# Attention in a fused kernel: value products in three blocks per pair of heads instead of five, and what uses their sums half a step later

## The chip, the cores and the metric

The kernel runs on one core of one Trainium2 chip. TensorE (PE), VectorE (DVE), ScalarE (ACT), GpSimd (POOL) and SyncE (SP, which issues DMAs) each work through their own instruction list in order; where one needs what another makes, it waits on a semaphore. The metric is the device time in microseconds (us) of one execution.

## The reference, cut to what matters

Attention with a bias computed from positions feeds a layer of experts and a gated layer. Only the attention is touched by the change.

```python
scores = scale * np.matmul(q, k.transpose(0, 1, 3, 2))      # 4 batches, 8 heads, 576 x 576
scores = scores + bias.transpose(2, 0, 1)[None, :, :, :]
scores = scores - np.max(scores, axis=-1, keepdims=True)
attn = np.exp(scores)
attn = attn / (np.sum(attn, axis=-1, keepdims=True) + 1e-09)
return np.matmul(attn, v).astype(np.float32)
...
x = np.ascontiguousarray(attn_out.transpose(0, 2, 1, 3)).reshape(B * S, H * D)
x = _moe_ref(x=x, **moe_kwargs)
return _moe2_ref(x=x, **moe2_kwargs)
```

## The kernel before

A first stage computes the bias and writes it to DRAM, the attention stage follows, and then come the experts and the gated layer. The attention works on pairs of heads, 16 of them: pair 0 to pair 15, four for each batch. A pair has five **steps** (0 to 4), one for each block of 115 query rows. The loop runs over `u` in twos; step k of pair P is `u = 10 P + 2 k`, so `u % 10 // 2` is k. Its code is written out in one order, and that order is the order on every engine. A step issues:

1. On PE the score products of the *next* step (`emit_qk`, 12 matmuls into two `sc` banks).
2. For the step itself the transposes of the weights after exp: four into bank `pa` and three into `pb` (`emit_T`); ACT copies both to the buffers `ptt` (`emit_pte`).
3. For the next step, on DVE, bias and row minimum (`emit_max`, two instructions at line 351, which read the `sc` banks), then on ACT two exps (`emit_exp`).
4. `service(u)`: one item of the list `fill`.
5. Value products from the list `avq`: so many blocks of keys as `AVN[k]` says.
6. Two more transposes into `pa`, once ACT has emptied it, and ACT's copy of them; the next step's four transposes into `pa` wait for this copy.
7. `service(u + 1)`: one more item of `fill`.

**Value products.** The rows of a pair are taken in two groups, g = 0 (230 rows, steps 0 and 1) and g = 1 (346 rows, steps 2 to 4). A group has five blocks of keys, c = 0 to 4 (`emit_av`, two products of 64 output rows each, into bank `av`); after the last one DVE copies the sum (line 397). Group 0 is queued at the end of step 1, group 1 at the end of step 4, so that it is worked off in steps 0 and 1 of the next pair. Behind its last block four items are put on `fill`:

- `x_back(P, 0)`: four transposes of the sums into bank `mi`, then on DVE two small operations on the row sums (lines 410, 411) and a multiply that reads `mi` (line 417).
- `x_back(P, 1)`: one transpose into `mi`, a multiply, and the DMAs of the result.
- `x_fwd(P, 0)`, `x_fwd(P, 1)`: four transposes and one, each with a copy on DVE (434, 437).

At step 4 `prep` puts items for the pair after next on `fill`: two times four transposes (`tr_main`, line 198, copied by DVE at 201 and 203), one transpose with the loads of later pairs (`tr_rem`), and two items that only POOL works on (`split_pair`: a copy, line 216, and a subtraction, line 218). There is one bank `mi`: each of these items waits until DVE has read what the one before left there.

**Where `fill` runs behind.** After the last pair of a batch three items for the router (`logits`) come in between, and one slot is given to the router's matmul. So in pairs 1 to 4, 8 and 12 `x_back(0)` stands at the end of step 1 (these are called *quick* pairs below), in pairs 5, 6, 9, 10, 13 and 14 at the end of step 2 (*late* pairs), in pairs 7 and 11 at the beginning of step 2 (*middle* pairs). The slots of a quick pair, two for each step: `tr_rem`, `split 0` | `split 1`, `x_back 0` | `x_back 1`, `x_fwd 0` | `x_fwd 1`, nothing | `tr_main 0`, `tr_main 1`.

The bias of a pair's two heads is read back from DRAM into `nb` by DMAs in the first pairs (`nb_load`); the loads for pair 3 are issued in pair 1, behind the other loads in SP's queue.

Of the kernel before, what the change touches and what calls it, by code (L numbers as in the profile page):

```python
# [19 lines left out]
B, H, S, D = 4, 8, 576, 64  # L20
# [9 lines left out]
NP = H // 2  # L30
# [17 lines left out]
def fused(ctx, tc, q, k, v, w1, b1, w2, wg, mw1, mw2, gw, vw, ow, rg, tab, cst, out):  # L48
# [21 lines left out]
    def bank(nm):  # L70
        return {"pa": ps_pt, "pb": ps_pt, "av": ps_av, "mi": ps_mi}[nm].tile([128, 512], F32, name=nm, tag=nm)
# [78 lines left out]
    with tc.manual_schedule():  # L150
# [24 lines left out]
        def load_pair(P):  # L175
            b, hp = divmod(P, NP)
            r = f0[:, 2 * S * (P % 2):2 * S * (P % 2) + 2 * S].rearrange("p (n h d) -> p n h d", h=2, d=D)
            for c, src in ((0, k), (1, q)):
                for i in range(2):
                    a = src[b, 2 * hp + i]  # L180
                    sy.dma_start(out=r[:, 4 * c:4 * c + 4, i], in_=bass.AP(a.tensor, a.offset, [[D, 128], [128 * D, 4], [1, D]]))
                    sy.dma_start(out=r[64 * c:64 * c + 64, 8, i], in_=a[512:576])
            raws[P] = r

        def load_v(P):
            b, hp = divmod(P, NP)
            vt = v_r[P % 3].rearrange("p (t h d) -> p t h d", h=2, d=D)
            for i in range(2):
                a = v[b, 2 * hp + i]
                sy.dma_start(out=vt[:, 0:4, i], in_=bass.AP(a.tensor, a.offset + 64 * D * i, [[D, 128], [128 * D, 4], [1, D]]))  # L190
                sy.dma_start(out=vt[64 * i:64 * i + 64, 4, i], in_=a[512 * (1 - i):512 * (1 - i) + 64])
            vts[P] = vt

        def tr_main(P, c):
            assert P == 0 or P - 1 in prepped
            p = bank("mi")
            for n in range(4):
                te.transpose(p[:, 128 * n:128 * n + 128], raws[P][:, 4 * c + n].rearrange("p h d -> p (h d)"), idF)
            o = kqf_r[P % 2][:, S * c:S * c + 512]
            if c == 0:  # L200
                ve.tensor_copy(o, p)
            else:
                ve.tensor_scalar(o, p, -0.125, None, ALU.mult)

        def tr_rem(P):
            p = bank("mi")
            te.transpose(p[:, 0:128], raws[P][:, 8].rearrange("p h d -> p (h d)"), idF)
            o = kqf_r[P % 2].rearrange("p (c s) -> p c s", c=2)
            ve.tensor_copy(o[:, 0, 512:576], p[:, 0:64])
            ve.tensor_scalar(o[:, 1, 512:576], p[:, 64:128], -0.125, None, ALU.mult)  # L210

        def split_pair(P, part):
            assert last_qk[0] >= 10 * P - 11
            x, kq = kqf_r[P % 2], kq_r[P % 2]
            if part == 0:
                ge.tensor_copy(kq[:, 0:2 * S], x)  # L216
            else:
                ge.tensor_tensor(kq[:, 2 * S:4 * S], x, kq[:, 0:2 * S].bitcast(F32), ALU.subtract)
                kqs[P] = [kq[:, S * c:S * c + S] for c in range(4)]
                prepped.add(P)  # L220

        def prep(P):
            return [
                lambda: tr_main(P, 0),
                lambda: tr_main(P, 1),
                lambda: (tr_rem(P), load_pair(P + 2) if 0 < P < B * NP - 2 else None, load_v(P) if P > 1 else None),
                lambda: split_pair(P, 0),
                lambda: split_pair(P, 1),
            ]


# [156 lines left out]
        def emit_av(P, g, c):  # L388
            n = NG[g]
            pt = pts[g]  # L390
            if c == 0:
                avs[P, g] = bank("av")
            a = avs[P, g]
            for i in range(2):
                te.matmul(a[64 * i:64 * i + 64, 0:n], vts[P][:, c, i], pt[8 if c == 4 else 4 * i + c], start=(c == 0), stop=(c == T - 1))  # L395
            if c == T - 1:
                ve.tensor_copy(xu_r[P % 2][:, NG[0] * g:NG[0] * g + n], a[:, 0:n])
                if g == 1:
                    fill.extend([lambda: x_back(P, 0), lambda: x_back(P, 1), lambda: x_fwd(P, 0), lambda: x_fwd(P, 1)])

        def fb(P, part):
            return "pa" if P == B * NP - 1 and part else "mi"
# [1 line left out]
        def x_back(P, part):  # L404
            b, hp = divmod(P, NP)
            r = P % 2
            t0, t1 = ((0, 4), (4, 5))[part]
            n = t1 - t0
            if part == 0:
                ve.tensor_scalar(rinv[:QP, r], sums[:QP, r], 1e-9, None, ALU.add)  # L410
                ve.reciprocal(rinv[:QP, r], rinv[:QP, r])
            xu = xu_r[r]
            xt = x_r[r].rearrange("p (t i d) -> p t i d", t=T, i=2)
            p = bank(fb(P, part))
            for t in range(t0, t1):
                te.transpose(p[:QP, 128 * (t - t0):128 * (t - t0) + 128], xu[:, QS * t:QS * t + QP], idF)
            ve.tensor_tensor(xt[:QP, t0:t1], p[:QP, 0:128 * n].rearrange("p (t i d) -> p t i d", t=n, i=2),
                             rinv[:QP, r, t0:t1].unsqueeze(3).to_broadcast([QP, n, 2, D]), ALU.mult)
            if part == 1:
                xt = x_r[r].rearrange("p (t d) -> p t d", t=T)  # L420
                dst = x_dr[b * S:(b + 1) * S, 128 * hp:128 * hp + 128]
                sy.dma_start(out=dst[0:T * QS].rearrange("(t p) d -> p t d", p=QS), in_=xt[:QS])
                sy.dma_start(out=dst[S - 1:S], in_=xt[QS:QP, T - 1])

        def x_fwd(P, part):
            b, hp = divmod(P, NP)
            xt = x_r[P % 2].rearrange("p (t d) -> p t d", t=T)
            o = xT[b % 2].rearrange("p (k s) -> p k s", s=S)[:, hp]
            p = bank(fb(P, part))
            pv = p.rearrange("p (c r) -> p c r", r=128)  # L430
            if part == 0:
                for t in range(4):
                    te.transpose(pv[:, t, 0:QP], xt[:QP, t], idF[:QP, :QP])
                ve.tensor_copy(o[:, 0:4 * QS].rearrange("p (t q) -> p t q", q=QS), pv[:, :, 0:QS])
            else:
                te.transpose(pv[:, 0, 0:QP], xt[:QP, 4], idF[:QP, :QP])
                ve.tensor_copy(o[:, 4 * QS:S], pv[:, 0, 0:QP])
                if hp == NP - 1:
                    sy.dma_start(out=xT_dr[b], in_=xT[b % 2])
                    fill.extend([lambda: logits(b), lambda: logits2(b, 0), lambda: logits2(b, 1)])  # L440
# [229 lines left out]
        U1 = 0  # L670
        EVD = ()
        FLN = (1,) * 10
        AVN = (3, 2, 2, 2, 1)
        fill, rq = [], []
        def service(u):
            Pn = u // 10 + 2
# [18 lines left out]
        for u in range(-2, NU, 2):  # L695
# [11 lines left out]
            service(u)  # L707
            for _ in range(min(len(avq), AVN[u % 10 // 2])):
                avq.pop(0)()
# [510 lines left out]
```

## Time and profile before

| what | value |
|---|---|
| time, median of 3 runs | 1095.11 us (1094.44 to 1096.6) |
| the profiled execution: its time, its span | 1097.88 us, 1096.1 us |
| bias stage, up to the first score products of pair 0 | 64.66 us |
| attention, up to the first product of the experts | 322.50 us; PE busy 310.04, ACT 219.66, DVE 201.84 |
| the rest | 708.94 us; PE busy 688.32 |
| granted TensorE clock, mean | 0.987 |

The span runs from the first to the last instruction. Busy is the time in which an engine has an instruction running; matmuls are pipelined and their ends are modelled, so that a stretch in which PE is busy throughout may still hold waits. A row of windows gives the stretch and its length, then the busy times of PE, of PE's weight loads, of DVE, ACT and POOL with the number of their instructions, then the granted clock, the share of the DMA engines and GB/s. In the trace a value product counts as two instructions. The length of a step is read from the start of its score products (line 344) to the start of the next step's.

### The profile page before, as it was taken

The page shows a single profiled execution, that of the slowest core. Times are in us where ns is not written, and L with a number is a line of the kernel's source. Part 1 is how long each engine was busy: PE and PEld are TensorE (multiplying, and loading weights), DVE is VectorE, ACT ScalarE, POOL GpSimd, SP SyncE. Part 2 cuts the span into 40 slices and gives each one's busy share as a digit, 9 for nine tenths or more (in the row PEclk, how much of TensorE's full clock was granted, in tenths as well). Part 3 has the DMA queues.
Part 4 walks back from the last instruction along what each step waited for, and adds up shares of the span by engine and source line. Part 5 has one row for each costly group of instructions (what it writes and reads, how often), then busy time and mean ns, then how long its engine had stood idle before and what let it go on. Part 6 is the DMA issues. An engine that isn't in the chain of part 4 may idle for free.

```text
span 1096.1 us, 18791 instructions
## 1 busy us (share of the span) xinstructions
PE 1051.1 (96%) x7136; PEld 870.3 (79%) x7136; DVE 630.5 (58%) x1377; ACT 511.5 (47%) x1141; POOL 275.9 (25%) x165
## 2 busy tenths in 40 slices
PE   7889899999999999999997999999999999999996
PEld 3366566666666687889887899999999999999996
DVE  8955456666656748431478566566466666333332
ACT  6667566776766734544454543333333333222221
POOL 4821221211211542634375311112112211000000
PEclk9989899999999999999998999999999999999999
DMA  5978633232333252655273243332122220011210
GB/s 144 288 225 204 166 69 96 58 76 88 72 101 95 76 190 67 198 208 203 93 220 108 76 129 121 123 111 98 69 68 80 75 97 30 1 58 70 89 44 32
DMA packets 109171, 120.97 MB, mean 110 GB/s; under 512 B 65970, under 2 KB 75314, under 8 KB 108562
## 3 DMA queue, kind: packets, MB, share of 16 engines
q1 hardware_dynamic: 108834, 118.92, 36.3%
q8 instruction: 58, 0.95, 0.4%
q0 software_dynamic: 240, 0.79, 0.2%
q14 instruction: 39, 0.32, 0.1%
HBM read 84.39 MB, written 35.28 MB: 109 GB/s over the span
## 4 chain that ended last, share of the span: by engine, by line
PE 77%; DVE 8%; DMA 4%; ACT 4%; issue 4%; SPq 2%; POOL 0%; DVEq 0%; ACTq 0%
PE sc L971 9%; PE sc L970 9%; PE sc L969 9%; PE av L395 6%; PE sc L828 6%; PE sc L344 6%; PE pa L369 5%; PE av L855 4%; PE sc L281 2%; DMA nb<-nb_dr 2%; PE mi L855 2%; PE av L990 2%; PE av L989 2%; PE av L988 2%; PE mi L988 1%
## 5 line engine op out<-in xcount | busy, mean ns | idle before, releaser
L969 PE MATMUL sc<-xng,mw 128*128 128x384 f32 x576 | 193.0, 335 | 0.0
L971 PE MATMUL sc<-xng,mw 128*128 128x384 f32 x576 | 192.7, 334 | 0.0
L970 PE MATMUL sc<-xng,mw 128*128 128x384 f32 x576 | 192.5, 334 | 0.0
L351 DVE CUSTOM_DVE_ANT_0 scx<-sc,nb 116x576 f32<-116x576 f32 x160 | 114.9, 755 | 69.5 <-PE sc L344 53.8
L974 ACT ACTIVATE f<-sc 128x384 f32<-128x384 f32 x72 | 35.5, 492 | 237.5 <-PE sc L971 236.5
L357 ACT ACTIVATE scx<-scx,cf 116x576 f32<-116x576 f32 x160 | 123.9, 785 | 3.5 <-DVE cf L351 3.5
L975 DVE TENSOR_TENSOR f<-f,sc 128x384 f32<-128x384 f32 x72 | 39.9, 555 | 138.2 <-ACT f L974 137.8
L383 ACT COPY ptt<-pa 128x460 f32<-128x460 f32 (+3 forms) x160 | 71.6, 448 | 99.3 <-PE pa L369 99.2
L969 PEld LDWEIGHTS sc<-xng,mw 128*128 128x128 f32 x576 | 108.2, 188 | 0.7
L970 PEld LDWEIGHTS sc<-xng,mw 128*128 128x128 f32 x576 | 108.2, 188 | 0.7
L971 PEld LDWEIGHTS sc<-xng,mw 128*128 128x128 f32 x576 | 108.1, 188 | 0.0
L828 PE MATMUL sc<-xhl,w1h 128*128 128x256 f32 (+1 forms) x512 | 92.8, 304 | 7.9 <-DVE hTh L836 7.0
L344 PE MATMUL sc<-kq 64*116 64x288 f32 x960 | 88.0, 313 | 3.9 <-DVE xT L457 2.3
L369 PEld LDWEIGHTS pa<-cf,scx 115*128 115x128 f32 (+1 forms) x480 | 49.1, 143 | 51.5 <-ACT ptt L383 26.1
L369 PE MATMUL pa<-cf,scx 115*128 115x115 f32 (+1 forms) x480 | 84.1, 285 | 3.6 <-ACT ptt L383 3.3
L828 PEld LDWEIGHTS sc<-xhl,w1h 128*128 128x128 f32 x512 | 78.9, 194 | 10.3 <-issue 7.6
L395 PE MATMUL av<-ptt,f 128*64 128x346 f32 (+1 forms) x512 | 86.0, 432 | 0.0
L344 PEld LDWEIGHTS sc<-kq 64*116 64x116 f32 x960 | 67.2, 179 | 18.5 <-issue 6.9
L216 POOL CAST kq<-kqf 128x1152 fp32r<-128x1152 f32 x16 | 18.5, 1154 | 245.2 <-DVE kqf L210 245.2
L977 DVE TENSOR_TENSOR mw<-f,xng 128x384 fp32r<-128x384 f32 x72 | 40.3, 559 | 42.0 <-ACT xng L976 42.0
L976 ACT CAST xng<-f 128x384 fp32r<-128x384 f32 x72 | 37.2, 517 | 45.9 <-DVE f L975 45.2
L395 PEld LDWEIGHTS av<-ptt,f 128*64 128x64 f32 x512 | 35.6, 137 | 28.3 <-issue 8.7
(305 smaller groups left out, 2132.5 us busy)
## 6 DMA issues: line engine op xcount, KB each, us to landing
st<-in_moe_w_dram SPq DMA_DIRECT2D x28, 512.0 KB
nb_dr<-nb SPq DMA_DIRECT2D x36, 295.5 KB
f<-xn_dr SPq DMA_DIRECT2D x12, 768.0 KB
cvt<-in_moe_w_gate_dram SPq DMA_DIRECT2D x12, 512.0 KB
cvt<-in_moe_w_val_dram SPq DMA_DIRECT2D x12, 512.0 KB
cvt<-in_moe_w_out_dram SPq DMA_DIRECT2D x12, 512.0 KB
nb<-nb_dr SPq DMA_DIRECT2D x24, 252.0 KB
xT_dr<-xT SPq DMA_DIRECT2D x4, 1152.0 KB
```

The lines of the kernel that those rows point to most:

```text
L344: te.matmul(p[i][:QP, j, 0:288], qq[64 * i:64 * i + 64, QS * t:QS * t + QP], kk[64 * i:64 * i + 64, 288 * j:288 * j + 288], start=(n == 0) ...
L351: ve.tensor_tensor_reduce(out=s2, in0=p[:QP, :, 0:288], in1=nbv(P % NP, t)[:QP, i].rearrange("p (a j) -> p a j", a=2), op0=ALU.add, op1=AL ...
L357: se.activation(out=s, in_=s, func=ACTF.Exp, scale=-1.0, bias=mx[:QP, u % 4:u % 4 + 1], accum_out=sums[:QP, P % 2, t, i:i + 1])
L369: te.transpose(pv[:, c], scx[:w, o:o + 128], idF[:w, :w])
L383: (ve.tensor_copy if (i, c0 % 4, k0) in EVD else se.copy)(bass.AP(d.tensor, d.offset + q0, [d.ap[0], [NG[g], k1 - k0], [1, w]]), pv[:, k0:k1])
L395: te.matmul(a[64 * i:64 * i + 64, 0:n], vts[P][:, c, i], pt[8 if c == 4 else 4 * i + c], start=(c == 0), stop=(c == T - 1))
L828: te.matmul(p[:, j, 0:n], w[:, c:c + 128], xx[:, S * kk + s0:S * kk + s0 + n], start=(kk == 0 and w is w1h and i == 0), stop=(kk == 3 and ...
L855: te.matmul(p, h, w, start=(f == 0 and i == 0), stop=(f == 7 and i == len(terms) - 1))
L969: te.matmul(p[:, i, 0:XT], a, h[:, kk], start=(kk == 0), stop=False)
L970: te.matmul(p[:, i, 0:XT], a, l[:, kk], start=False, stop=False)
L971: te.matmul(p[:, i, 0:XT], al, h[:, kk], start=False, stop=(kk == 3))
L977: ve.tensor_tensor(gTl[:, c], g, gTh[:, c].bitcast(F32), ALU.subtract)
```

## The change

There are three edits. `AVN` now gives the five blocks of group 1 to steps 0 and 1 as before (3 and 2), none to step 2, all five blocks of group 0 to step 3, and none to step 4; so a pair has three runs of value products instead of five. Both parts of `split_pair` become one item of `fill`. Where a pair's sums are complete, an empty item is put ahead of the four that use them, in all pairs but the last; the number of items of a pair stays as it was.

```diff
@@ prep
-                lambda: split_pair(P, 0),
-                lambda: split_pair(P, 1),
+                lambda: (split_pair(P, 0), split_pair(P, 1)),
@@ emit_av
-                    fill.extend([lambda: x_back(P, 0), lambda: x_back(P, 1), lambda: x_fwd(P, 0), lambda: x_fwd(P, 1)])
+                    fill.extend([lambda: None] * (P < B * NP - 1) + [lambda: x_back(P, 0), lambda: x_back(P, 1), lambda: x_fwd(P, 0), lambda: x_fwd(P, 1)])
@@
-        AVN = (3, 2, 2, 2, 1)
+        AVN = (3, 2, 0, 5, 0)
```

The slots of a quick pair are now: `tr_rem`, both splits | nothing, empty item | `x_back 0`, `x_back 1` | `x_fwd 0`, `x_fwd 1` | `tr_main 0`, `tr_main 1`. In a late pair `x_back 0` and `x_back 1` stand on both sides of the value products of step 3, and `x_fwd 0` and `x_fwd 1` in step 4.

The rows below are PE's list, with the operation, output bank, inputs, output size and count; line numbers of the changed kernel are one lower from line 228 on. The first place is a quick pair from the value products of step 1 on (64x346) to step 3. Before:

```order
L395 MATMUL av<-ptt,f_90 64x346 x4
L369 MATMUL pa<-cf,scx 128x115 x2
L416 MATMUL mi<-cf,scx 116x128 x4
L344 MATMUL sc<-kq 116x288 x12
L369 MATMUL pa<-cf,scx 128x115 x4
L369 MATMUL pb<-cf,scx 128x115 x3
L416 MATMUL mi<-cf,scx 116x128
L395 MATMUL av<-ptt,f_90 64x230 x4
L369 MATMUL pa<-cf,scx 128x115 x2
L433 MATMUL mi<-cf,scx 128x116 x4
L344 MATMUL sc<-kq 116x288 x12
```

After the change:

```order
L394 MATMUL av<-ptt,f_90 64x346 x4
L368 MATMUL pa<-cf,scx 128x115 x2
L343 MATMUL sc<-kq 116x288 x12
L368 MATMUL pa<-cf,scx 128x115 x4
L368 MATMUL pb<-cf,scx 128x115 x3
L415 MATMUL mi<-cf,scx 116x128 x4
L368 MATMUL pa<-cf,scx 128x115 x2
L415 MATMUL mi<-cf,scx 116x128
L343 MATMUL sc<-kq 116x288 x12
L368 MATMUL pa<-cf,scx 128x115 x4
L368 MATMUL pb<-cf,scx 128x115 x3
L432 MATMUL mi<-cf,scx 128x116 x4
```

The two items of `x_back` (L416, now L415) have moved into step 2, on both sides of the two transposes into `pa`, and the value products between them (64x230) are gone from there. The second place is the same pair from step 3 into step 4. Before:

```order
L395 MATMUL av<-ptt,f_90 64x230
L395 MATMUL av<-scx,f_90 64x230
L395 MATMUL av<-ptt,f_90 64x230
L395 MATMUL av<-scx,f_90 64x230
L369 MATMUL pa<-cf,scx 128x115 x2
L344 MATMUL sc<-kq 116x288 x12
L369 MATMUL pa<-cf,scx 128x116 x4
L369 MATMUL pb<-cf,scx 128x116 x3
L198 MATMUL mi<-cf,f_90 128x128 x4
L395 MATMUL av<-f_90 64x230 x2
L369 MATMUL pa<-cf,scx 128x116 x2
L198 MATMUL mi<-cf,f_90 128x128 x4
```

After the change:

```order
L394 MATMUL av<-ptt,f_90 64x230 x5
L394 MATMUL av<-scx,f_90 64x230
L394 MATMUL av<-ptt,f_90 64x230
L394 MATMUL av<-scx,f_90 64x230
L394 MATMUL av<-f_90 64x230 x2
L368 MATMUL pa<-cf,scx 128x115 x2
L435 MATMUL mi<-cf,scx 128x116
L343 MATMUL sc<-kq 116x288 x12
L368 MATMUL pa<-cf,scx 128x116 x4
L368 MATMUL pb<-cf,scx 128x116 x3
L198 MATMUL mi<-cf,f_90 128x128 x4
L368 MATMUL pa<-cf,scx 128x116 x2
```

Group 0 now has all its ten products in one run in step 3, and in step 4 only two transposes into `pa` lie between the two items of `tr_main` (L198). The third place is pair 5, a late pair, from the score products of step 2 to the value products of step 3. Before:

```order
L344 MATMUL sc<-kq 116x288 x12
L369 MATMUL pa<-cf,scx 128x115 x4
L369 MATMUL pb<-cf,scx 128x115 x3
L395 MATMUL av<-ptt,f_90 64x230 x4
L369 MATMUL pa<-cf,scx 128x115 x2
L416 MATMUL mi<-cf,scx 116x128 x4
L344 MATMUL sc<-kq 116x288 x12
L369 MATMUL pa<-cf,scx 128x115 x4
L369 MATMUL pb<-cf,scx 128x115 x3
L416 MATMUL mi<-cf,scx 116x128
L395 MATMUL av<-ptt,f_90 64x230
```

After the change:

```order
L343 MATMUL sc<-kq 116x288 x12
L368 MATMUL pa<-cf,scx 128x115 x4
L368 MATMUL pb<-cf,scx 128x115 x3
L368 MATMUL pa<-cf,scx 128x115 x2
L343 MATMUL sc<-kq 116x288 x12
L368 MATMUL pa<-cf,scx 128x115 x4
L368 MATMUL pb<-cf,scx 128x115 x3
L415 MATMUL mi<-cf,scx 116x128 x4
L394 MATMUL av<-ptt,f_90 64x230 x5
L394 MATMUL av<-scx,f_90 64x230
```

Step 2 has neither value products nor an item for PE any more: between its seven transposes and the two into `pa` stands nothing.

## Rows read from the trace of the kernel before

**Rows 1.** Windows (stretch, length, busy by engine, PEclk, DMA), pair 7, steps 1-4.
```profile
216.30:219.78 3.48, 3.48 (x30) 2.19 (x29) 2.02 (x7) 2.14 (x7) 2.80 (x2) 1.00 0.29 67
219.78:223.85 4.07, 3.86 (x36) 2.73 (x36) 2.73 (x8) 3.37 (x10) 0.99 (x1) 1.00 0.56 127
223.85:227.44 3.59, 3.59 (x36) 2.69 (x35) 2.29 (x6) 2.13 (x6) 0.00 (x0) 1.00 0.23 58
227.44:231.31 3.87, 3.79 (x34) 2.73 (x33) 2.63 (x7) 2.94 (x8) 0.00 (x0) 1.00 0.22 51
```

**Rows 2.** Timeline (start, length, engine, line), PE, pair 7, step 2.
```profile
219.78 1.05 PE L344 MATMUL sc<-kq 64*116 64x288 f32 x12
...
220.76 0.61 PE L369 MATMUL pa<-cf,scx 115*128 115x115 f32 x4
...
221.51 0.60 PE L416 MATMUL mi<-cf,scx 128*116 128x128 f32 x4
...
222.04 1.00 PE L395 MATMUL av<-ptt,f 128*64 128x230 f32 x8
...
222.97 0.41 PE L369 MATMUL pa<-cf,scx 115*128 115x115 f32 x2
...
223.59 0.32 PE L416 MATMUL mi<-cf,scx 128*116 128x128 f32 x1 [0.21 <-DVE scx L417]
```

**Rows 3.** Timeline of DVE in the same step.
```profile
221.66 0.75 DVE L351 CUSTOM_DVE_ANT_0 scx<-sc,nb 116x576 f32<-116x576 f32 x1
...
222.85 0.69 DVE L417 TENSOR_TENSOR scx<-mi,cf 116x512 f32<-116x512 f32 x1
```

**Rows 4.** Timeline of all engines, step 4 of pair 7.
```profile
229.69 0.61 PE L395 MATMUL av<-f 128*64 128x230 f32 x4
...
229.99 0.69 DVE L201 COPY kqf<-mi 128x512 f32<-128x512 f32 x1
...
230.23 0.42 PE L369 MATMUL pa<-cf,scx 116*128 116x116 f32 x2
...
230.73 0.66 PE L198 MATMUL mi<-cf,f 128*128 128x128 f32 x4
```

**Rows 5.** Windows, pair 1, steps 1 to 4.
```profile
93.58:97.88 4.30, 4.14 (x34) 2.58 (x33) 2.26 (x7) 2.96 (x9) 2.66 (x2) 1.00 1.06 293
97.88:101.49 3.61, 3.61 (x35) 2.68 (x34) 2.34 (x6) 2.08 (x6) 0.00 (x0) 1.00 1.04 230
101.49:104.68 3.19, 3.19 (x31) 2.28 (x31) 2.27 (x6) 2.19 (x7) 0.00 (x0) 1.00 1.13 187
104.68:108.67 3.99, 3.83 (x34) 2.73 (x34) 2.44 (x6) 3.23 (x10) 0.00 (x0) 1.00 0.71 111
```

**Rows 6.** Timeline of PE, steps 2 and 3 of pair 0.
```profile
79.85 0.61 PE L369 MATMUL pa<-cf,scx 115*128 115x115 f32 x4 [0.68 <-ACT ptt L383]
...
80.69 1.00 PE L395 MATMUL av<-ptt,f 128*64 128x230 f32 x8
...
83.21 0.61 PE L369 MATMUL pa<-cf,scx 115*128 115x115 f32 x4 [0.21 <-ACT ptt L383]
```

**Rows 7.** Windows, pair 5: steps 0 and 1, then steps 2 and 3.
```profile
173.25:181.94 8.69, 8.60 (x73) 5.58 (x72) 5.25 (x18) 5.95 (x19) 0.10 (x1) 1.00 0.08 18
181.94:189.14 7.20, 7.20 (x69) 5.28 (x68) 6.57 (x18) 5.45 (x15) 3.69 (x2) 1.00 0.46 105
```

**Rows 8.** Timeline of POOL in the bias stage.
```profile
42.18 2.73 POOL L218 TENSOR_TENSOR kq<-kqf,kq 128x1152 fp32r<-128x1152 f32 x1
```

**Rows 9.** Windows: step 4 of pair 2, step 0 of pair 3.
```profile
123.92:130.88 6.96, 4.33 (x34) 3.03 (x33) 2.44 (x6) 3.92 (x12) 0.00 (x0) 0.88 0.46 118
130.88:137.42 6.54, 6.54 (x35) 4.11 (x34) 2.49 (x7) 2.58 (x7) 2.39 (x2) 0.60 0.56 130
```

**Rows 10.** Timeline, last load of the bias of pair 3, its reader.
```profile
119.49 0.25 SPq L300 DMA_DIRECT2D nb<-nb_dr  x1
...
128.41 0.76 DVE L351 CUSTOM_DVE_ANT_0 scx<-sc,nb 116x576 f32<-116x576 f32 x1 [2.55 <-DMA nb<-nb_dr]
```

## The prediction

> **What bounds the kernel now.** I read the windows by stage first: the change touches only the attention. There PE is busy nearly all the time, but a busy PE says little, so I went on to the timeline of PE step by step, and then to the timelines of DVE and ACT wherever PE's rows name one of them as the releaser. Three limits stand close together.
>
> PE's own work. In step 3 of pair 7 PE is busy for all of 3.59 us, in step 1 for all of 3.48 [rows 1]. The pieces of a step come out of the starts in one of them [rows 2]: score products 0.98 us (219.78 to 220.76), seven transposes 0.75 (to 221.51), four transposes of an item 0.53 (to 222.04), value products of two blocks 0.93 (to 222.97). One block takes 0.54 (229.69 to 230.23) [rows 4]; so a block of group 0 costs 0.39, and each run of blocks has a fixed 0.15 beside it. Two transposes into `pa` take 0.25 ahead of more transposes; an item of one transpose takes 0.2 to 0.26.
>
> ACT's round. From the four transposes into `pa` of one step to those of the next ACT empties `pa` and `pb`, makes two exps and empties `pa` again. In pair 0 this round alone sets the step: 79.85 to 83.21 is 3.36 us, and PE waits for ACT before both ends, although two blocks of value products lie in between (80.69) [rows 6]. So no step can be much under 3.36, whatever PE has in it.
>
> DVE's chain through the one bank `mi`. Where two items of `fill` that use `mi` stand in the same step, the second waits until DVE has read the first, and DVE first does the two minima of the next step. In step 2 of pair 7, with both items of `x_back`, the second minimum starts at 221.66, the multiply at 222.85 and ends at 223.54 [rows 3]; PE's one transpose starts at 223.59, having idled [rows 2], and the step takes 4.07 us [rows 1]. In step 4, with both items of `tr_main`, DVE's copy runs from 229.99 to 230.68 and PE's second four transposes start at 230.73 [rows 4]; the step takes 3.87 [rows 1]. Both chains hang on the score products at the step's start, not on the value products.
>
> **The change part by part.** The value products themselves stay the same in number and length. What changes is in which step they stand, and which limit that step has.
>
> *Quick pairs.* The new order has exact forerunners in pair 7. Step 1 loses `x_back 0` (and the wait for DVE's copy of the sum) and is like step 1 of pair 7 as far as PE goes: 4.30 [rows 5] becomes 3.48 [rows 1], a gain of 0.82. Step 2 gets both items of `x_back`, as pair 7 has them. The value products that leave it lay inside the wait for DVE, so 3.61 [rows 5] becomes 4.07 [rows 1], and PE idles about 1.1 us in it. Step 3 has the items of pair 7's step 3, and three blocks more: 3.59 + 3 x 0.39 = 4.76 against 3.19, a loss of 1.57. Step 4 loses one block, which also lay inside DVE's chain: 3.87 against 3.99, a gain of 0.12. Step 0 stays. Sum: -0.82 + 0.46 + 1.57 - 0.12 = **+1.1 us a pair**. For pairs 1 to 3 this is 3.3. In 4, 8 and 12 the items for the router follow, one slot later too, and their copies on DVE may hide a part; between 0 and 1.1 I take the middle, 1.6 for the three.
>
> *Late pairs* (six). Steps 0 and 1 only exchange items of the same kind: 8.69 [rows 7] stays, to 0.1. Step 2 is left with score products and transposes alone. PE is through with it after 0.98 + 0.75, a wait until ACT has emptied `pa` (0.5 at most), and 0.3 to 0.4 for the last two transposes and the change to score products: some 2.6 us, but the next step's transposes into `pa` can't start before 0.98 + 3.36 = 4.34 from its beginning [rows 2, 6]. After them step 3 has 0.75 + 0.53 + 5 x 0.39 + 0.15 + 0.25 + 0.2 = 3.83, with 0.05 for the changes between kinds 3.9. Steps 2 and 3 together: 8.2 against 7.20 [rows 7], **+1.0**. What was hidden behind ACT's round in step 2 is in the open in step 3. Step 4 with both items of `x_fwd` is again one of DVE's chain, 3.4 to 3.5, much as before. Six pairs: 6.0. If ACT's round did not hold PE at all, the two steps would take 2.6 + 0.98 + 3.9 = 7.5 and the pair lose 0.3; those are the bounds, 0.3 and 1.0, and rows 6 speak for the upper one.
>
> *The rest.* The two middle pairs have `x_back` around the boundary of steps 2 and 3 now; between 0 and 1.0 each I take 0.6, since step 3 gets all five blocks as elsewhere: 1.2. Pair 0 has no `x_back`: step 2 stays at ACT's round, step 3 gets 1.17, step 4 gives 0.2 back: 0.9. Pair 15 gains 0.8 in step 1, loses 0.5 in step 2 and about 0.7 in step 3, at whose end ACT was awaited before: 0.3.
>
> *The splits.* POOL's subtraction now follows its copy at once. The values are needed a step and a half later, so nothing waits. In the bias stage the subtraction of pair 0, 2.73 us, goes ahead of two of POOL's bias products [rows 8]; they are used two groups later. I take 0, with 2.7 as the upper bound. Fewer runs of value products save 2 x 0.15 a pair on PE, which is in the sums above.
>
> *One wait that shrinks.* The second minimum for pair 3 waits 2.55 us for a load of the bias, until 128.41 [rows 10]. SP issued the last of these loads at 119.49 [rows 10]; its place in the program is the end of step 3 of pair 1, which PE reached at 104.68 [rows 5]. SP's queue is some 15 us behind and not waiting for the attention, so the landing stays where it is. Until then the changed kernel has fallen behind by 0.9 + 1.1 + 1.2 (pair 2 up to step 3) = 3.2 us, and the wait is gone: step 4 of pair 2 takes 3.87 in place of 6.96, a gain of 3.1 [rows 9, 1]. [...] Bounds for both together: 0 and 5.5; I take 5.5, because the delay is larger than the wait.
>
> Sum: 3.3 + 1.6 + 6.0 + 1.2 + 0.9 + 0.3 - 5.5 = **+7.8 us**. (Pair 2's step 4 is counted with the wait, which takes 0.1 off.) The profiled execution took 1097.88 us, 2.8 over the median of 1095.11; laid on the median, the forecast is 1102.9, **1103 us**.
>
> **A rule that speaks for the change.** Each run of value products costs a fixed 0.15 us beside its blocks [rows 2, 4]; two runs fewer in 16 pairs are worth 2 x 0.15 x 16 = 4.8 us where PE sets the pace. [...]
>
> **Rivals.** *Faster, because PE sets the pace.* If the waits for DVE and ACT moved along with the work, the runs would give their 4.8 us and the quick pairs the wait in step 1 (4.30 - 3.48 - 0.53 + 0.1 [rows 5, 1, 2], about 0.4 each): 4.8 + 6 x 0.4 = 7.2 us, 1088. For it speaks PE's busy share; against it that steps of this make exist in pair 7 with the wait in them. It decides if steps 2 and 4 of quick pairs come out below 3.5. *No change:* ACT's round doesn't hold PE after an emptied step; then late pairs lose 0.3, middle pairs and those with the router's items nothing, and the sum is 7.8 - 6 x 0.7 - 1.2 - 1.6 = +0.8. Against it: rows 6, and that ACT can't begin a step's copies before PE's transposes. *Slower by more:* the landing moves with the attention, or the clock falls all the same; 7.8 + 2.4 to 5.5 gives 1105 to 1108. *The clock falls in new places:* the new waits of about 1.1 us are less than half of the 2.55 after which it fell here, and 0.68 [rows 6] did nothing; if it fell twice more, each at 2.4 us, 1108. [...]
>
> **How the numbers follow.** Forecast 1103 (1098 to 1107): 0.62. Landing or clock as before, 1105 to 1108: 0.14. New falls of the clock, 1107 and more: 0.05. No change: 0.09. Faster: 0.10. A difference under 0.2% (2.2 us) can't be told from none in this kernel. That gives 0.82 slower, 0.08 the same, 0.10 faster. Leaving out the faster cases, part of the unchanged ones and the far end, the range is 1097 to 1110.
>
> **What would show it.** Steps from score products to score products: in quick pairs about 4.2, 3.5, 4.1, 4.8, 3.9 us; in late pairs steps 2 and 3 together 8.2, with PE held before the transposes into `pa` of step 3 by ACT; PE's single transpose of `x_back 1` held by DVE's multiply in step 2; no wait for the load of the bias at 128 us, and the clock at full around it. The prediction is wrong if step 2 shrinks by what the value products took, or if step 3 grows by less than three blocks.

## The result, and the profile after

The changed kernel takes 1109.84 us (median; 1106.62 to 1110.05, one disturbed execution left out of this range and of the ratio) against 1094.78 before. The ratio, of the means, is 1.0126, 95% interval 1.0101 to 1.015, so 13.8 us or 1.3% slower; the medians are 15.1 us apart. The forecast was 1103, 1097 to 1110.

The profiled execution of the changed kernel took 1109.62 us, close to its median; its span is 1107.8 us at a mean clock of 0.995 (0.987 before). The attention goes from 64.86 to 398.11, 333.25 us in place of 322.50, and what follows takes 709.69 in place of 708.94. From profile to profile the loss is 11.7 us.

Windows of pair 1, steps 1 to 4, which answer to [rows 5]:

```profile
91.88:95.36 3.48, 3.48 (x31) 2.20 (x30) 1.68 (x5) 2.15 (x7) 2.66 (x2) 1.00 0.84 207
95.36:99.42 4.06, 2.90 (x27) 2.24 (x27) 2.72 (x8) 3.35 (x10) 0.00 (x0) 1.00 1.06 247
99.42:104.18 4.76, 4.76 (x48) 3.55 (x47) 2.62 (x7) 2.63 (x7) 0.00 (x0) 1.00 1.07 238
104.18:108.91 4.73, 3.29 (x31) 2.53 (x30) 2.48 (x7) 3.11 (x8) 0.00 (x0) 1.00 0.78 120
```

Steps 1 to 3 are 3.48, 4.06 and 4.76, to 0.1 what was forecast. In step 2 PE is busy for only 2.90 of 4.06 us; in step 3 it is busy throughout. Step 4, 4.73 here, is 3.88 in pair 3; the difference is a wait that comes up below. The timeline of PE in step 2 of the same pair answers to [rows 2]:

```profile
97.08 0.60 PE L415 MATMUL mi<-cf,scx 128*116 128x128 f32 x4
97.59 0.42 PE L368 MATMUL pa<-cf,scx 115*128 115x115 f32 x2
99.17 0.32 PE L415 MATMUL mi<-cf,scx 128*116 128x128 f32 x1 [1.16 <-DVE scx L416]
```

and that of DVE to [rows 3]:

```profile
97.22 0.75 DVE L350 CUSTOM_DVE_ANT_0 scx<-sc,nb 116x576 f32<-116x576 f32 x1
...
98.42 0.69 DVE L416 TENSOR_TENSOR scx<-mi,cf 116x512 f32<-116x512 f32 x1
```

DVE's chain (minimum, small operations, multiply) runs from the score products as it did before; PE reaches the single transpose earlier and waits 1.16 us for the multiply. Where two blocks of value products lay inside that chain, there is now nothing.

Windows of pair 5, steps 0 and 1, then 2, then 3, answer to [rows 7]:

```profile
173.14:181.78 8.64, 8.64 (x74) 5.66 (x74) 5.22 (x15) 5.17 (x15) 0.00 (x0) 1.00 0.08 18
...
181.78:184.35 2.57, 2.23 (x22) 1.70 (x21) 2.12 (x9) 1.43 (x7) 1.62 (x2) 1.00 0.25 57
184.35:189.95 5.60, 4.90 (x48) 3.56 (x47) 5.13 (x12) 4.12 (x11) 2.18 (x1) 1.00 0.49 108
```

and the timeline of PE in steps 2 and 3 says what holds step 3:

```profile
182.76 0.61 PE L368 MATMUL pa<-cf,scx 115*128 115x115 f32 x4
...
184.35 1.06 PE L343 MATMUL sc<-kq 64*116 64x288 f32 x12
186.11 0.62 PE L368 MATMUL pa<-cf,scx 115*128 115x115 f32 x4 [0.70 <-ACT ptt L382]
```

Steps 0 and 1 stay at 8.64. The emptied step 2 takes 2.57, and PE then waits for ACT before the transposes into `pa`, which start 186.11 - 182.76 = 3.35 us after those of step 2: ACT's round of 3.36 [rows 6]. Both steps together take 8.17, forecast 8.2.

Three of the steps 4 wait for a load of the bias now. DVE's second minimum in them, in pairs 0, 1 and 2 (timeline of DVE):

```profile
85.71 0.76 DVE L350 CUSTOM_DVE_ANT_0 scx<-sc,nb 116x576 f32<-116x576 f32 x1 [0.69 <-ACT ptt L382]
...
106.90 0.76 DVE L350 CUSTOM_DVE_ANT_0 scx<-sc,nb 116x576 f32<-116x576 f32 x1 [0.78 <-DMA f<-in_q_dram]
...
128.20 0.76 DVE L350 CUSTOM_DVE_ANT_0 scx<-sc,nb 116x576 f32<-116x576 f32 x1 [0.86 <-PE pa L368]
```

and the windows of step 4 of pair 2 and step 0 of pair 3, which answer to [rows 9]:

```profile
125.39:130.21 4.82, 3.29 (x31) 2.54 (x31) 2.51 (x7) 3.12 (x8) 0.00 (x0) 1.00 0.53 129
130.21:136.00 5.79, 5.79 (x35) 3.39 (x35) 2.49 (x7) 2.57 (x7) 2.58 (x2) 0.71 0.49 116
```

The third wait ends at 128.20, where it ended at 128.41 before [rows 10]: the landing did stay. But PE comes to this step at 125.39, only 1.47 us later than before (123.92), not 3.2. The releasers in the brackets (ACT, PE, another load) are not what was missing: without the loads these waits are gone, as the run with the bias of pair 0 shows below. And the clock still fell once, to 0.71 in step 0 of pair 3 (0.60 before).

In pair 14 step 3 takes 6.59 us, a us more than in the other late pairs. The timeline of DVE and POOL there, and of PE's last item:

```profile
369.02 2.64 POOL L218 TENSOR_TENSOR kq<-kqf,kq 128x1152 fp32r<-128x1152 f32 x1
...
369.71 0.15 DVE L513 TENSOR_SCALAR cf<-cf 128x1 int32<-128x1 f32 x1
369.77 1.92 DVE L515 TENSOR_SCALAR cf<-cf 128x8 f32<-128x8 f32 x1
...
372.46 2.37 POOL L608 TENSOR_TENSOR w1l<-xT,w1h 128x1024 fp32r<-128x1024 f32 x1 [0.79 <-ACT w1h L607]
...
372.96 1.93 DVE L517 TENSOR_TENSOR cf<-cf 128x40 f32<-128x40 f32 x1
...
375.31 0.69 DVE L416 TENSOR_TENSOR x_b<-mi,cf 116x512 f32<-116x512 f32 x1
...
376.06 0.32 PE L415 MATMUL mi<-cf,scx 128*116 128x128 f32 x1 [0.78 <-DVE x_b L416]
```

Two small operations of the router, of 8 and 40 elements in a row, last 1.9 us on DVE and end 0.03 and 0.06 us after POOL's subtraction; one of a single element (L513) takes 0.15 beside the same subtraction. The second of the two delays `x_back 0`'s multiply, and PE waits 0.78 us for it.

### The profile page after: what moved, and what is told of

It reads as the page before. It is cut to its first block, busy times and chain, and to the rows that moved or that the text cites. A ratio compares the mean times of both kernels' runs of the same rounds, so it can differ in the third digit from the quotient of the medians.

```text
span 1107.8 us, 18770 instructions
## 1 busy us (share of the span) xinstructions
PE 1041.5 (94%) x7136; PEld 868.2 (78%) x7136; DVE 641.3 (58%) x1377; ACT 512.0 (46%) x1141; POOL 275.1 (25%) x165
## 4 chain that ended last, share of the span: by engine, by line
PE 76%; DVE 9%; DMA 5%; ACT 4%; issue 4%; SPq 2%; POOL 0%; DVEq 0%; ACTq 0%; POOLq 0%
PE sc L970 9%; PE sc L968 9%; PE sc L969 9%; PE av L394 7%; PE sc L827 5%; PE sc L343 5%; PE pa L368 4%; PE av L854 4%; PE sc L280 2%; PE mi L854 2%; DMA nb<-nb_dr 2%; PE av L989 2%; PE av L988 1%; PE av L987 1%; PE mi L987 1%
## 5 line engine op out<-in xcount | busy, mean ns | idle before, releaser
L343 PE MATMUL sc<-kq 64*116 64x288 f32 x960 | 85.0, 307 | 1.6 <-DVE cf L350 1.0
L394 PE MATMUL av<-ptt,f 128*64 128x346 f32 (+1 forms) x512 | 82.7, 432 | 0.0
```

The costliest lines, as they stand in the source:

```text
L343: te.matmul(p[i][:QP, j, 0:288], qq[64 * i:64 * i + 64, QS * t:QS * t + QP], kk[64 * i:64 * i + 64, 288 * j:288 * j + 288], start=(n == 0) ...
```

## The experiments

Each expectation letters its own theories. In e1 to e4 theory A is that of the prediction: the value products lay inside waits (for DVE in step 2, for ACT in step 2 of late pairs) and now lie outside them. The prediction's faster rival, that PE sets the pace and fewer runs are a gain, is answered by e1 too.

**Only the order of the value products (e1).** The kernel before, with

```diff
-        AVN = (3, 2, 2, 2, 1)
+        AVN = (3, 2, 0, 5, 0)
```

> The kernel before with the new numbers of value blocks (3, 2, 0, 5, 0) alone; the items of fill stay as before. Theory A (the steps that are emptied are held by ACT's round or by DVE's chain through the bank mi, so the blocks moved to step 3 are in the open): late pairs take 8.2 us for steps 2 and 3 (before 7.2), quick pairs 3.4 and 4.4 (before 3.6 and 3.2), middle pairs 4.1 and 4.8; in all 10 to 13 us over the kernel before, 1105 to 1108 us. Theory B (what costs is that the users of the sums come half a step later): this kernel is within 3 us of the one before, 1095 to 1098 us.

Measured: 1110.6 us, ratio 1.0153 (1.0129 to 1.0178). Step 2 of pair 1, then step 4 of pair 2 and step 0 of pair 3 (windows):

```profile
98.45:101.88 3.43, 2.96 (x28) 2.20 (x28) 2.34 (x6) 1.90 (x6) 0.00 (x0) 1.00 1.05 269
...
126.36:130.22 3.86, 3.29 (x31) 2.53 (x31) 2.24 (x6) 2.53 (x6) 0.00 (x0) 1.00 0.53 121
130.22:134.38 4.16, 4.16 (x35) 2.56 (x34) 2.40 (x7) 2.95 (x10) 1.13 (x1) 1.00 0.48 115
```

Step 2 loses a run of two blocks, 0.93 us of work [rows 2], and only 0.18 of time; step 3 goes from 3.19 to 4.35, three blocks at 0.39. Late pairs take 3.02 + 5.11 = 8.13 in steps 2 and 3, middle pairs 4.06 + 4.76. B falls, A holds for the steps; the total is above what A gave, by some 3 to 7 us. From profile to profile it is 11.9 us (1109.82 against 1097.88), as A gave; the rest is that the profiled execution of the kernel before stood 3.6 us over the median of these runs, 1094.31, and that of e1 0.8 under its own. The last two rows are worth noting: this kernel reaches step 4 of pair 2 at 126.36, 2.4 us later than before, and there both the wait and the fall of the clock are gone, 6.96 - 3.86 = 3.10 and 6.54 - 4.16 = 2.38 us, together the 5.5 that the prediction took for the changed kernel. (The last load was also issued 2.1 us earlier here, at 117.36 against 119.49 [rows 10].)

**Only the items (e2).** The changed kernel with `AVN = (3, 2, 2, 2, 1)`.

> The changed kernel with the old numbers of value blocks (3, 2, 2, 2, 1): only the users of the sums half a step later and the two splits in one item. Theory A: the steps of a quick pair are 4.2, 3.5, 4.1, 3.6, 3.9 us, in sum as before to 0.1; late pairs lose about 0.4 each, because step 2 is at ACT's round and step 3 has both items of x_back with only 0.9 us of value products between them; 1 to 4 us over the kernel before, 1096 to 1099 us. Theory B: nearly all of the loss is here, 1105 to 1110 us.

Measured: 1098.01 us, ratio 1.0035 (1.0023 to 1.0046). Quick pairs take 4.16, 3.48, 4.06, 3.59, 3.87 us, the items' share as forecast: 0.82 gained in step 1, 0.46 lost in step 2, 0.4 lost in step 3. Most of the loss is thus the runs'; the two do not add up (3.8 and 16.7 us against 13.8). Both totals hold more than the steps: e1 is rid of the waits for the bias, while e2's trace has 6.80 us in step 4 of pair 0, 6.51 in that of pair 2, and 4.0 us more than before in pair 14. In the other late pairs the items alone cost 0.4 to 0.9 us and the runs alone 1.0 to 1.2, but both together only 1.1 to 1.2; why they overlap there is not shown.

**The run of five in step 2 (e3).** The changed kernel with `AVN = (3, 2, 5, 0, 0)`, which puts the run behind the first item of `x_back`, inside DVE's chain.

> The changed kernel with the five blocks of group 0 in step 2 instead of step 3 (3, 2, 5, 0, 0): three runs as well. Theory A: in quick pairs the run lies between the two items of x_back, so that DVE's chain is hidden; step 2 takes 4.9 us and step 3, with both items of x_fwd, 3.45 by DVE's chain, 8.35 in place of 8.8; late pairs 4.2 and 4.1, as after the change to 0.1; in all 2 to 4 us faster than the changed kernel, 1106 to 1108 us. Theory C (a run of five costs the same in the open wherever it stands): the time of the changed kernel, within 1 us of 1110.

Measured: 1109.86 us, ratio 1.0144 (1.0121 to 1.0166): no gain, A's total missed. The steps are A's all the same (windows of pair 1, steps 2 and 3):

```profile
96.48:101.29 4.81, 4.81 (x47) 3.54 (x46) 3.06 (x9) 3.34 (x10) 0.00 (x0) 1.00 1.05 222
101.29:104.76 3.47, 2.96 (x27) 2.25 (x26) 2.34 (x7) 2.13 (x6) 0.00 (x0) 1.00 1.15 250
```

8.28 in place of 8.82, so some 3.2 us less in the six quick pairs. The waits for the bias and the clock behind them take 0.9 of it back: step 4 of pair 0 takes 5.90, step 0 of pair 1 5.57 at a clock of 0.72, step 4 of pair 2 5.43. More goes elsewhere: pair 14 takes 23.07 us, 1.7 more than in the changed kernel, and the other late pairs 0.1 to 0.3 more each. In all the attention is 0.4 us shorter (332.90 against 333.25). What follows it took 712.50 in place of 709.67 in this execution; no edit touches that part.

**`x_back 1` in another bank (e4).** The changed kernel with

```diff
-            p = bank(fb(P, part))
+            p = bank("pb" if part and P < B * NP - 1 else fb(P, part))
```

> The changed kernel with the second item of x_back in bank pb, which ACT has emptied by then, so that it need not wait for DVE to read mi. Theory A: step 2 of a quick pair falls from 4.06 to 3.4 us, where ACT's round holds it (3.36 from one set of transposes into pa to the next), steps 2 and 3 from 8.8 to 8.1; the first pairs give a part of it back to the loads of the bias; late pairs unchanged; 3 to 5 us faster than the changed kernel, 1105 to 1107 us. Rival (the bank is not what PE waits for in step 2): unchanged, 1109 to 1111 us.

Measured: 1104.61 us, ratio 1.0098 (1.0082 to 1.0115), near what A gave. Step 2 of quick pairs falls from 4.06 to 2.83; step 3 rises from 4.76 to 5.29, since PE then waits for ACT's round (timeline of PE, pair 1, and pair 7 below it):

```profile
98.47 0.62 PE L368 MATMUL pa<-cf,scx 115*128 115x115 f32 x4 [0.47 <-ACT ptt L382]
...
225.90 0.32 PE L415 MATMUL pb<-cf,scx 128*116 128x128 f32 x1 [0.74 <-ACT ptt L382]
```

So it is the one bank `mi`, and not DVE as such, that makes step 2 long; and behind it stands ACT's round. In middle pairs the item is the first of its step, `pb` is not empty yet, and step 3 gets 0.96 longer. Step 3 of pair 14 takes 5.60 here in place of 6.59: its wait for DVE, too, went through `mi`.

**The bias waits taken out of both kernels (e5, e6).** Pairs 1 to 3 read the bias of pair 0, which is in SBUF early; their output is another one, all transfers and instructions stay.

```diff
-... in1=nbv(P % NP, t)[:QP, i] ...
+... in1=nbv(P % NP if P >= NP else 0, t)[:QP, i] ...
```

The kernel before:

> The kernel before, with pairs 1 to 3 reading the bias of pair 0, which is in SBUF early (the loads of the other biases still run; the output of those pairs is another one). What is tested is the term of the forecast that was 5.5 us: the wait for the load of the bias in step 4 of pair 2 and the fall of the clock behind it. Theory A (the steps themselves cost 13 to 15 us, and the changed kernel gets back 1.4 to 3 us of it because it waits less for the bias): the wait of 2.6 us and the clock's fall go, steps 4 of pair 2 and 0 of pair 3 take 4.0 and 4.2 in place of 7.0 and 6.5; 1089 to 1091 us. Theory B (that wait is no loss, since the stage behind it catches up): as before, 1094 to 1096.

The changed kernel:

> The changed kernel with the same edit: pairs 1 to 3 read the bias of pair 0. Theory A: the three waits of 0.7 to 0.9 us in steps 4 of pairs 0, 1 and 2 go, and the clock's fall in step 0 of pair 3 (1.6 us); step 4 of pairs 0 and 1 takes 3.9 in place of 4.6 to 4.7; 1105 to 1107 us, and the distance to the kernel before with the same edit is that of the steps alone, 15 to 17 us. Theory B: as the changed kernel, 1109 to 1110. Theory C (the steps are worth the forecast 13.3 us and the rest of the miss is in the bias loads): a distance of 13 to 14 us, so 1103 to 1104.

Measured: 1089.24 us, ratio 0.9952 (0.994 to 0.9964), and 1103.47, ratio 1.0087 (1.0065 to 1.011), both against the kernel before. Step 4 of pair 2 and step 0 of pair 3 (windows), first of the kernel before with the edit:

```profile
123.29:127.27 3.98, 3.83 (x34) 2.73 (x33) 2.44 (x6) 3.22 (x10) 0.00 (x0) 1.00 0.51 120
127.27:131.43 4.16, 4.16 (x35) 2.56 (x34) 2.40 (x7) 3.05 (x10) 1.13 (x1) 1.00 0.53 121
```

then of the changed kernel with it, with step 4 of pair 0 ahead:

```profile
83.00:86.87 3.87, 3.28 (x30) 2.53 (x29) 2.30 (x6) 2.54 (x6) 0.00 (x0) 1.00 0.92 261
...
123.72:127.60 3.88, 3.29 (x31) 2.54 (x31) 2.42 (x7) 2.55 (x6) 0.00 (x0) 1.00 0.50 135
127.60:131.76 4.16, 4.16 (x35) 2.56 (x34) 2.40 (x7) 2.93 (x10) 1.13 (x1) 1.00 0.51 115
```

In the kernel before, the waits and the clock behind them are worth 6.96 + 6.54 - 3.98 - 4.16 = 5.36 us in the trace and 5.0 in the time. In the changed kernel they are worth 0.76 + 0.86 + 0.94 (steps 4 of pairs 0, 1, 2) + 1.63 (clock) = 4.2 in the trace, 4.3 by the two ratios. The change gives back about 1 us of the 5.5 forecast. With the waits out of both, the kernels are 1103.47 - 1089.24 = 14.2 us apart, 14.8 by the two ratios; the forecast's steps had 13.3, and those of the two traces, the bracketed terms of the table below, add up to 15.4. The steps are those of theory A of the second expectation, its time is that of C, and the distance lies between the two: the times do not decide.

**The loads issued earlier (e9, e10).** The bias of pair 3 is asked for 6 and 8 half steps earlier; that of pair 2 stays where it was, at u = 4 and 7, other than the expectations say. The values are loaded ahead of the next pair's queries:

```diff
-                lambda: (tr_rem(P), load_pair(P + 2) if 0 < P < B * NP - 2 else None, load_v(P) if P > 1 else None),
+                lambda: (tr_rem(P), load_v(P) if P > 1 else None, load_pair(P + 2) if 0 < P < B * NP - 2 else None),
...
-            if 4 <= u < 24 and u % 10 in (4, 7):
-                nb_load((u + 6) // 10 + 1, 0, T, (u - 4) % 10 // 3)
+            if u in (4, 7, 8, 9):
+                nb_load(2 + (u > 7), 0, T, int(u in (7, 9)))
```

The kernel before:

> The kernel before with the loads of the bias of pairs 2 and 3 issued 5 to 9 half steps earlier, and the load of the values ahead of that of the next pair's queries. Theory A (the landing follows SP's queue): the last load lands before it is wanted at 125.9 us, the wait of 2.6 us and the clock's fall behind it go, 1089 to 1091 us. Theory B (the landing is set by the sum of the bytes, whatever their order): the wait moves to another load of the queue, 1093 to 1096.

The changed kernel:

> The changed kernel with the same edit of the loads. Theory A: the waits of 0.7 to 0.9 us in steps 4 of pairs 0 to 2 shrink or go, no fall of the clock in step 0 of pair 3; 1105 to 1108 us. Theory B: no change, 1109 to 1110.

Measured: 1089.3 us, ratio 0.9961 (0.9946 to 0.9975), and 1105.57, ratio 1.0103 (1.0081 to 1.0125). In the first, step 4 of pair 2 and step 0 of pair 3 have neither the wait nor a fall of the clock; two smaller waits appear earlier (4.92 in step 4 of pair 1, 4.23 in step 2 of pair 2). Windows of steps 4 of pairs 1 and 2 and step 0 of pair 3:

```profile
102.80:107.72 4.92, 3.87 (x36) 2.74 (x35) 2.44 (x6) 3.91 (x12) 0.00 (x0) 1.00 1.06 239
...
123.63:127.62 3.99, 3.84 (x35) 2.74 (x34) 2.44 (x6) 3.23 (x10) 0.00 (x0) 1.00 0.70 154
127.62:131.79 4.17, 4.17 (x36) 2.57 (x36) 2.40 (x7) 3.04 (x10) 1.14 (x1) 1.00 0.50 113
```

In the second, step 4 of pair 2 takes 3.86 and step 0 of pair 3 4.17, while 0.8 us of the wait in step 4 of pair 1 stays (4.67). That is theory A in both. The landing follows SP's queue, as [rows 10] were read (e9 issues the last of these loads at 105.79, the kernel before at 119.49), and the kernel before has about 4 us to win there, whatever becomes of the change.

**Only the split as one item (e12).** The kernel before, with an empty item in the second one's place:

```diff
-                lambda: split_pair(P, 0),
-                lambda: split_pair(P, 1),
+                lambda: (split_pair(P, 0), split_pair(P, 1)),
+                lambda: None,
```

> The kernel before with only one of the three edits: both parts of the split are one item (an empty item stands in the second one's place, so that no other item moves). The one instruction that moves is POOL's subtraction of pair 0 in the bias stage, which now comes ahead of two of POOL's bias products. What is tested: every run profiled so far without this edit has PE at half clock at the start of the attention (from about 68 us, 3.4 to 10.2 us long), no run with it does. Theory A (the edit itself is what keeps the clock up): no fall there, score products of pair 0 start 1.6 to 2.3 us earlier than in the kernel before, 1091 to 1093 us, or less where the waits for the bias take it. Theory B (the fall comes with something else, or not in most executions): as before, 1094 to 1095. Nothing here speaks for slower.

Measured: 1094.14 us, ratio 1.0001 (0.9989 to 1.0013), where A had a gain. The windows from 67 to 79 us, of the kernel before:

```profile
67.00:79.00 12.00, 10.88 (x63) 8.76 (x63) 5.67 (x16) 6.48 (x18) 0.90 (x1) 0.57 0.64 172
```

and of this one, with step 4 of pair 0 and of pair 2 and step 0 of pair 3:

```profile
67.00:79.00 12.00, 9.53 (x86) 7.11 (x88) 7.25 (x20) 8.89 (x25) 3.78 (x2) 1.00 0.60 165
81.98:87.51 5.53, 3.88 (x35) 2.75 (x35) 2.44 (x6) 4.00 (x12) 0.00 (x0) 1.00 1.03 274
...
123.75:129.72 5.97, 3.86 (x34) 2.73 (x34) 2.44 (x6) 3.90 (x12) 0.00 (x0) 1.00 0.49 124
129.72:133.89 4.17, 4.17 (x36) 2.57 (x35) 2.40 (x7) 2.47 (x7) 1.14 (x1) 1.00 0.46 108
```

The clock stays up: from the first score products to the end of step 0 of pair 0, and in its step 1, the kernel takes 7.12 + 2.63 in place of 9.44 + 4.01, 3.7 us less; and steps 4 of pairs 0 and 1 give 1.44 and 1.70 of it back, waiting for the loads, so that step 4 of pair 2 begins 0.2 us earlier than before (123.75 against 123.92). There it waits a us less (5.97 against 6.96) and keeps the clock behind it (4.17 against 6.54): at the end of step 0 of pair 3 this trace is 3.5 us ahead (133.89 against 137.42). Yet the medians are equal, so the two profiles do not stand for the other executions. Whether it is the edit that keeps the clock up, or the fall is missing in most executions of either kernel (theory B), is not settled: of the 14 profiles the fall is in all four without the edit and in one of ten with it, the run e14 below (clock from 67 to 79 us: 0.57, 0.57, 0.58 and 0.86 without it; 0.59 in e14, 1.00 in the other nine).

**Both, and a second bank (e13, e14).** e13 is e9 with the split as one item; e14 also lets the second item of `tr_main` (pairs 0 to 3, 7, 11) and `x_back 1` (pairs 7, 11) write into `pb`, where they stand in a step's second slot.

> The kernel before with the early loads of the bias, and the two parts of the split as one item as well. With theory A of the run with the split alone: 1087 to 1088.5 us, since the early loads alone had 1089.3 and a fall of 3.4 us at the start of the attention. With B: 1089 to 1090.

> The same, and the second of two items of one step writes into the bank pb in place of mi, where it stands in a step's second slot: the second item of tr_main in step 4 of pairs 0 to 3, 7 and 11, the second of x_back in step 2 of pairs 7 and 11. Theory A (DVE's chain through the one bank sets these steps): step 4 becomes 3.5 to 3.7 in place of 3.9 to 4.1, step 2 of pairs 7 and 11 becomes 3.6 in place of 4.06; 2 to 3 us less than the same kernel without it, 1085 to 1087. Theory B (ACT's round or PE's own work stands right behind that chain): under 1 us.

Measured: e13 1090.56 us, ratio 0.9965 (0.9952 to 0.9978); e14 1088.81, ratio 0.9962 (0.9947 to 0.9976). Steps 2 and 4 of pair 7 in e14 (windows), against 4.07 and 3.87 in [rows 1]:

```profile
212.72:216.36 3.64, 3.64 (x36) 2.69 (x35) 2.64 (x8) 2.93 (x8) 0.99 (x1) 1.00 0.27 61
219.95:223.53 3.58, 3.58 (x36) 2.73 (x35) 2.63 (x7) 2.65 (x8) 0.00 (x0) 1.00 0.47 104
```

In the middle pairs the steps are as A gave; in pairs 1 to 3 step 4 only goes from 3.98 to 3.81. Some 2 us less in the steps do not show in the ratio, which is that of e9 within the interval: e13 came out nearest B, and A's total for e14 was missed by 2 us. e9, e13 and e14 beat both kernels, the one before by 4 us, and cannot be told apart.

**POOL's subtraction half a step earlier (e15).** The changed kernel, with the first of the experts' splits moved in pair 14:

```diff
-            pre.setdefault(PJ0 + PJS * i // 4, []).append(pj)
+            pre.setdefault(PJ0 + PJS * i // 4 - (i == 0), []).append(pj)
```

> The changed kernel with the first of the expert's splits (ACT's or DVE's copy and POOL's subtraction of 1024 columns) issued half a step earlier in pair 14. Tested is why step 3 of pair 14 takes 6.6 us, where the other late pairs take 5.6: in it one small DVE operation of the router's item lasts 1.93 us in place of 0.2, and ends when POOL's subtraction ends. Theory A (POOL's subtraction holds the small operation): with the subtraction elsewhere the long operation is gone from there or is another one, step 3 of pair 14 takes 5.6 and the time is 1 us less. Theory B (the step is long for another reason, its items alone): 6.5 to 6.6 as before.

Measured: 1109.79 us, ratio 1.0146 (1.0123 to 1.0169), and step 3 of pair 14 takes 8.15 us: A's numbers for time and step are wrong. Its mechanism is not (timeline of DVE and POOL):

```profile
367.74 0.22 DVE L515 TENSOR_SCALAR cf<-cf 128x8 f32<-128x8 f32 x1
370.17 2.36 POOL L608 TENSOR_TENSOR w1l<-xT,w1h 128x1024 fp32r<-128x1024 f32 x1 [20.76 <-ACT w1h L607]
370.25 2.33 DVE L517 TENSOR_TENSOR cf<-cf 128x40 f32<-128x40 f32 x1
...
372.47 1.15 POOL L216 CAST kq<-kqf 128x1152 fp32r<-128x1152 f32 x1
372.51 1.14 DVE L409 TENSOR_SCALAR cf<-cf 116x10 f32<-116x10 f32 x1
```

L515, now with POOL idle, takes 0.22 us in place of 1.92; L517 comes 0.08 us after the moved subtraction and lasts as long as it, and L409, 0.16 us elsewhere, lasts as long as POOL's cast. The step got longer by other things too: PE waits 1.55 us for ACT at its start, and the clock is down to 0.60 from 370.4 to 374.0.

## Why the prediction was right, and where its sizes were off

Direction and mechanism were right: the steps came out as laid down, and the two bounds (DVE's chain through `mi`, ACT's round) are those that e4 and the wait at 186.11 show. "So no step can be much under 3.36" is too strong as it stands: step 2 of pair 5 takes 2.57. What holds is the distance of 3.35 from one set of four transposes into `pa` to the next, and by that the late pairs were reckoned. Of the rivals, the faster one falls with e1, and the one without ACT's round with step 3 of pair 5. That the time still lies in the range, 0.16 us below its end, is luck: it is above 1108, the slowest case that the prediction worked out, and 2 to 3 us of its distance from the forecast come from the execution that the sum was laid on (below).

Term by term, forecast against the trace (after less before; in brackets e6 less e5, where no load is waited for):

| term | forecast | trace |
|---|---|---|
| pairs 1 to 3, steps alone | +3.3 | [+3.34] |
| pairs 4, 8, 12 | +1.6 | +1.52 [+1.53] |
| late pairs 5, 6, 9, 10, 13 | +5.0 | +5.86 [+5.95] |
| late pair 14 | +1.0 | +2.76 [+2.78] |
| middle pairs | +1.2 | +1.37 [+1.01] |
| pair 0, steps 2 to 4 | +0.9 | [+0.93] |
| pair 15 | +0.3 | -0.23 [-0.19] |
| waits for the bias and clock behind | -5.5 | -1.2 |
| pair 0, steps 0 and 1 (with the start of pair 0) | 0 | -3.5 |
| behind the attention | 0 | +0.75 |

**The step that failed** is "I take 5.5, because the delay is larger than the wait". The landing stayed at 128.2, as argued, and e1 shows that a kernel that comes 2.4 us later waits for nothing and keeps its clock (step 4 of pair 2 in 3.86, step 0 of pair 3 in 4.16 us at 1.00). The 5.5 is 3.1 for the wait [rows 9, 1] and 2.4 for the clock behind it, which the slower rivals use too; no run before the prediction shows that 2.4, and what the runs showed in its place is 6.54 [rows 9] against 4.16 in e1 and e5, 2.38 us. But the changed kernel came only 1.47 us later: from the first score products to the end of step 1 of pair 0 it took 9.75 us in place of 13.45, since the clock did not fall at the start of the attention (1.00 from 67 to 79 us, 0.57 before), and so met the loads for pairs 1 and 2 too, which the kernel before never waited for. The trace of e12 shows this by itself: 3.7 us won at the start, 0.2 left on reaching step 4 of pair 2. The waits and the clock behind them thus gave back 1.2 us in place of 5.5. The rival in which the clock falls all the same came nearer to the time than the forecast. In this pair of traces the 3.5 us won at the start, which the prediction had at 0, make up for most of the 4.3 missing here; what is left of the miss is mostly the late pairs, 2.6.

**Mis-sized:** late pairs have 0.17 more each, most of it in step 4 of pairs 5, 9 and 13 (3.60 against 3.33); and pair 14 has 1.0 us in step 3 for the small operations that last as long as POOL's, and 0.67 in step 4. The prediction took 14 for a late pair like the others, though the router and the experts' splits run there.

These terms add up to 11.6 us, within 0.1 of the 11.7 from profile to profile, which is 3.9 over the forecast. The +0.75 behind the attention says little: no edit touches that part, and in the 14 profiles it takes 706.0 to 712.5 us. The remaining 2 to 3 us are where the sum was laid on the median: the profiled execution of before stood 3.1 us over its median and had the lowest mean clock, 0.987, where the others that were measured with the experiments had 0.988 to 0.997; that of the changed kernel stood at its median. Which stretches ran slower in it only is not shown, since the other executions left no trace; that the fall of the clock at the start is missing in most of them would fit e12, and stays open.

**The fixed price of a run.** A run of five blocks takes 2.09 us in step 3 of pair 1, 5 x 0.39 + 0.15: the fixed price stands. Saving two of them per pair won next to nothing, because PE waited behind them: in e1 step 2 of pair 1 loses 0.93 us of work and 0.18 of time.

**Clock.** PE's waits of 1.16 to 1.18 us, one in each quick pair, did nothing to the clock (1.00 in all windows of 5 us from 60 to 400 but that from 130 to 135, 0.66); it fell in step 0 of pair 3, to 0.71, behind a wait of 1.53, and not behind those of 1.36 and 1.45 in steps 4 of pairs 0 and 1 (timeline of PE, changed kernel):

```profile
87.13 0.66 PE L198 MATMUL mi<-cf,f 128*128 128x128 f32 x4 [1.36 <-DVE kqf L201]
...
108.32 0.66 PE L198 MATMUL mi<-cf,f 128*128 128x128 f32 x4 [1.45 <-DVE kqf L201]
...
129.62 0.66 PE L198 MATMUL mi<-cf,f 128*128 128x128 f32 x4 [1.53 <-DVE kqf L201]
```

In e12 PE idled 1.65, 1.82 and 2.11 us in the same three steps (length less busy time in the windows: 5.53 - 3.88, 5.69 - 3.87, 5.97 - 3.86), and the clock stood at 1.00 in each of them and in step 0 of pair 3. So the length of one gap does not tell here which is followed by a fall, and what does is not shown.

## What to carry to other kernels

Before moving work out of a step, ask what that step waits for: work of 0.93 us that lay inside DVE's chain cost only 0.18 there (e1), and three blocks at 0.39 cost their full 1.16 in step 3 (3.19 to 4.35), where PE had no wait. A transfer that lands at a fixed time (here 128.41 us before and 128.20 after) is a post in the schedule: what is won ahead of it can go into a longer wait there, and what is lost can be hidden in a shorter one, so a gain or loss there is counted only after asking how far from the post the changed kernel arrives. And a forecast laid on one profiled execution inherits what was special in that execution, so its mean clock is worth a look first.

## What the runs showed of the hardware that was not expected

Some small DVE operations on SBUF lasted as long as a POOL operation that was running: 1.92 us (8 elements in a row, TENSOR_SCALAR, 0.22 alone) and 1.93 and 2.33 (40 elements, TENSOR_TENSOR, 0.2 in the kernel before) beside a subtraction, 1.14 (10 elements, TENSOR_SCALAR, 0.16 elsewhere) beside a cast, each ending 0.03 to 0.06 us after it. Not all did: one TENSOR_SCALAR of a single element (L513) took 0.15 beside a subtraction. The minima at line 350, which read the `sc` banks in PSUM, kept their 0.75 us beside the same subtractions. That it is the POOL operation that holds them e15 shows by moving it: L515, with POOL idle, took 0.22, L409 was held in its place (1.14), and L517 was held by the subtraction that was moved ahead of it (2.33). Why these operations are held and the others are not is not shown.
